# B's weights in fewer, larger loads ahead of GpSimd's compute, and a reordered start, in a four-layer kernel on one core

## The chip, the cores and the metric

One of the eight cores of a Trainium2 chip runs the kernel. The metric is the time of one execution in device microseconds (us), and the number that counts is the median of several runs. Where the text says TensorE, VectorE, ScalarE, GpSimd and SyncE, the profile says PE (and PEld for its weight loads), DVE, ACT, POOL and SP.

## The reference, cut to what matters

Four residual layers run over 2048 rows of 576 numbers: A, B, A, B, with the same weights for both A and for both B. A is attention over a sliding window (8 positions at a distance of 2, 32 heads of 18). B is a recurrence over 64 segments of 32 rows: each segment attends to itself and to 8 memory rows, and the first 8 output rows become the memory of the next segment.

```python
def _B_ref(x, mem0, Wq, Wk, Wv, Wo, seg_len):        # H = 32 heads, Dh = 128
    mem = mem0
    for s in range(n_seg):                            # 64 segments, one after the other
        h = concatenate([mem, x[s * 32:(s + 1) * 32]])
        q, k, v = h @ Wq, h @ Wk, h @ Wv              # 40 rows, 32 heads
        p = softmax(mask(q @ k.T * scale))
        o = einsum("bhte,hed->btd", p @ v, Wo)
        mem = o[:M]
        outs.append(o[M:])

x = x + _A_ref(_layernorm(x), A_wqkv, A_wo)
x = x + _B_ref(_layernorm(x), B_mem0, B_Wq, B_Wk, B_Wv, B_Wo, B_seg_len)
x = x + _A_ref(_layernorm(x), A_wqkv, A_wo)
x = x + _B_ref(_layernorm(x), B_mem0, B_Wq, B_Wk, B_Wv, B_Wo, B_seg_len)
```

All inputs are bf16.

## The kernel before, in words

**Tiling.** A works on tiles of 64 rows (`a_tile`, 32 tiles in each of two layers). B works in 69 steps (`b_step`): step t computes segment t of the first B layer (lane 0) and segment t - 5 of the second (lane 1) in the same matmuls. Each tile of the first A layer feeds two segments of lane 0, and so on, so that all four layers run interleaved.

**Weights.** B's weights stay in SBUF: `wq`, `wk`, `wv` hold rows 0 to 511 of 576, `wqk_r` holds the last 64 rows of both wq and wk, `wv_r` those of wv, and `wo` the output weights; together they are 18.9 MB. A's weights do not fit beside them. They are cut into 12 strips (9 of `A_wqkv`, three each for q, k and v, and 3 of `A_wo`). For the first tile, the strips are loaded into the memory that later holds B's `wo` (L498); so `wo` can only be loaded when tile 0's output projection (L680) has read them. The next two times a strip is needed, it is gathered again from the input, into one of three `ring` buffers; the second of these is also copied to DRAM, and later tiles fetch that copy (L508). A strip is gathered by two DMAs (L504: rows 0 to 511, 512 pieces; L505: the remainder, 64 rows for `A_wqkv`, 128 for `A_wo`).

**What sets the order.** Every operation is given to a planner (`_Plan`) with an engine, a duration, a priority, what it depends on and which buffers it takes. `_Plan.run` walks through a modelled time: on each engine it picks the ready operation with the lowest priority number, and so writes each engine's order of instructions. The engines then run their own lists strictly in order, and wait on semaphores. A planned time has no other effect on the chip. `LAT` and `START` are the planner's assumed latencies and starting times, `PR` its priorities. In the kernel before, B's weight loads are operations of an own queue of the planner, "SWQ": their instructions are issued by GpSimd, but the planner lets a weight load start only when the one before it has moved, and puts it into GpSimd's list at that place, among GpSimd's compute.

**The start.** `setup` first fills constants: GpSimd makes masks and patterns (L298 to L341), VectorE clears tiles (L301 to L401). Then, in the planner's order: SP issues the first x tile (L528), four strips, `B_mem0` (L443) into the same buffer x0, the other eight strips, and the second x tile (L528), again into x0, which must first have been read by the transposes of mem0 (L447). TensorE transposes x (L533), computes LayerNorm's sums (L471), tile 0's q, k and v (L570, 75 matmuls), the logits (L619), then transposes the second x, spreads tile 0's weights (L644), projects tile 0 (L680), and starts step 0 of B with queries and keys (L830 and L833, 27 matmuls for three heads), values (L877), scores (L909 to L919), the product with v (L960) and the projection with `wo` (L984). Tile 1's q, k and v (L570, from the ring) stand in TensorE's list between groups of step 0.

Of the kernel before, what the change touches and what calls it, by code (L numbers as in the profile page):

```python
# [10 lines left out]
ACT = mybir.ActivationFunctionType  # L11
# [5 lines left out]
P = 128  # L17
# [7 lines left out]
NH = 32  # L25
D = 576
T = 64
NS = T // SEG
AH = 32
# [5 lines left out]
EPS = 1e-5  # L35
# [16 lines left out]
class _Plan:  # L52
# [7 lines left out]
    LAT = {"PE": 0.22, "ACT": 0.08, "DVE": 0.08, "POOL": 0.08, "SP": 2.8, "SWQ": 2.2, "NONE": 0.0}  # L60
    SWITCH = 0.1
    PAGE, AHEAD, FETCH, POS = 256, 64, 4.1, 63
    START = {"POOL": 6.0, "SWQ": 6.0, "DVE": 2.5, "ACT": 2.2, "SP": 0.8}
# [183 lines left out]
class _K:  # L247
# [37 lines left out]
    def setup(self):  # L285
        nc, tc = self.nc, self.tc
# [14 lines left out]
        nc.vector.tensor_copy(out=ident4[:].rearrange("p (a b) -> p a b", a=4), in_=ident[:, 0:32].unsqueeze(1).to_broadcast([P, 4, 32]))  # L301
        self.ones = ones = cp.tile([P, P], BF16, name="ones")
        nc.vector.memset(ones[:], 1.0)
        self.ones_h = ones_h = cp.tile([P, P], BF16, name="ones_h")
        nc.vector.memset(ones_h[0:64, :], 1.0)
        nc.vector.memset(ones_h[64:128, :], 0.0)
        self.epsb = epsb = cp.tile([P, 1], F32, name="epsb")
        nc.vector.memset(epsb[:], EPS)
# [9 lines left out]
        et = epadT[0:AH]  # L318
# [6 lines left out]
        for q4 in range(1, 4):  # L325
            nc.vector.tensor_copy(out=epadT[q4 * AH:(q4 + 1) * AH], in_=et)
# [22 lines left out]
        nc.vector.memset(wo[:, NH * D:NH * D + 64], 0.0)  # L349

        st = wo[64:128, 0:9 * 1280].rearrange("p (a b) -> p a b", b=1280).rearrange("p (a c) b -> p a c b", c=3)
        nc.vector.memset(st[:, :, 0:2, 1024:1280], 0.0)
        nc.vector.memset(st[:, :, 2, 512:640], 0.0)
        nc.vector.memset(wo[:, 11 * 1280:12 * 1280], 0.0)
        self.mem0T = mem0T = cp.tile([P, 6, NM], BF16, name="mem0T")
        nc.vector.memset(mem0T[:], 0.0)
# [3 lines left out]
        def tiles(name, n, shape, dt=BF16):  # L360
            ts = [wp.tile(shape, dt, name=f"{name}{i}") for i in range(n)]
            self.pl.pool(name, ts)
            return ts
# [16 lines left out]
        for t_ in tiles("x0", 1, [P, 640]):  # L380
            nc.vector.memset(t_[0:T, D:640], 0.0)
            nc.vector.memset(t_[T:P, :], 0.0)
        tiles("xs", 1, [P, 5, 2, T])
        tiles("st", 1, [P, 2, T], F32)
        for t_ in tiles("xn", 1, [P, 5, T]):
            nc.vector.memset(t_[64:128, 4, :], 0.0)
# [13 lines left out]
        for t_ in tiles("ring", 3, [P, 5 * 256]):  # L400
            nc.vector.memset(t_[64:128, :], 0.0)  # L401
        pp = self.pool("psum", 1, space=PSUM)
        self.pl.pool("r", [pp.tile([P, 512], F32, name=f"r{i}") for i in range(8)])

    def pre(self):
        self.strip_in, self.strip_n = {}, {}

    def prologue(self):

        nc, pl = self.nc, self.pl  # L410
        for name, us in (("xnb1", 0.3), ("hT", 0.4), ("qk", 0.35), ("em", 0.35), ("ex", 0.45), ("fin", 0.3), ("xnb3", 0.3)):
            bufs = [pl.buf(name) for _ in pl.pools[name]]
            o = pl.op("NONE", 0.0, None, -30.0, acq=bufs)
            for b in bufs:
                pl.op("DVE", us, lambda e, b=b: nc.vector.memset(b.t[:], 0.0), -2.5, [o], uses=[b])

        def load(out, in_, mb):
            return pl.op("SWQ", mb / 0.36, lambda e: nc.gpsimd.dma_start(out=out, in_=in_), -20.0)
        o = None
        self.w_in = [[None] * 4 for _ in range(3)]  # L420
        src = (self.B_Wq, self.B_Wk, self.B_Wv)
        for ws in ((0, 1), (2,)):
            for i in ws:
                wr = self.Wb[i][1]
                for hf in range(2):
                    if i < 2:
                        out, in_ = wr[i * 64:(i + 1) * 64, hf * 16 * P:(hf + 1) * 16 * P], src[i][512:576, hf * 16:(hf + 1) * 16]
                    else:
                        out, in_ = wr[hf * 64:(hf + 1) * 64, :], src[i][512:576, hf * 16:(hf + 1) * 16]
                    o = load(out, in_.rearrange("p h e -> p (h e)"), 0.26)  # L430
            for n in range(4):
                for i in ws:
                    w4 = self.Wb[i][0]
                    o = self.w_in[i][n] = load(w4[:, :, n * 1024:(n + 1) * 1024], src[i][0:512, n * 8:(n + 1) * 8].rearrange(
                        "(k p) h e -> p k (h e)", k=4), 1.05)
        self.wo_in = []
        for n in range(4):
            o = load(self.wo[:, n * 8 * D:(n + 1) * 8 * D].rearrange("p (h d) -> p h d", h=8),
                     self.B_Wo[n * 8:(n + 1) * 8].rearrange("h e d -> e h d"), 1.18)
            self.wo_in.append(o)  # L440

        x0, ps = pl.buf("x0"), pl.buf("r")
        a = pl.op("SP", 0.5, lambda e: nc.sync.dma_start(out=x0.t[0:NM, 0:D], in_=self.B_mem0[0]), -2.0, acq=[x0])  # L443

        def tr(e):
            for c in range(5):
                nc.tensor.matmul(ps.t[:, c * NM:(c + 1) * NM], lhsT=x0.t[0:NM, c * P:(c + 1) * P], rhs=self.ident[0:NM, 0:NM],  # L447
                                 start=True, stop=True)
        b = pl.op("PE", 0.3, tr, -2.0, [a], acq=[ps], uses=[x0], mode="R", mm=5)

        def cp(e):
            nc.vector.tensor_copy(out=self.mem0T[:, 0:4, :], in_=ps.t[:, 0:4 * NM].rearrange("p (c n) -> p c n", c=4))
            nc.vector.tensor_copy(out=self.mem0T[0:64, 4, :], in_=ps.t[0:64, 4 * NM:5 * NM])
            nc.vector.tensor_copy(out=self.mem0T[64:128, 5, :], in_=ps.t[0:64, 4 * NM:5 * NM])
        self.mem0_in = pl.op("DVE", 0.6, cp, -2.0, [b], uses=[ps])
# [34 lines left out]
    def wload(self, i, src, rows, col0, n, prio, dep):  # L490
# [3 lines left out]
        pl, dma = self.pl, self.nc.sync.dma_start  # L494
        step, last = rows
# [6 lines left out]
        def gather(e):  # L502
            f, v, r, m = src[0:1, col0:col0 + 1], view(), min(P, src.shape[0] - last), min(n, src.shape[1] - col0)
            dma(out=v[:, 0:4, 0:m], in_=bass.AP(f.tensor, f.offset, [[src.shape[1], P], [step * src.shape[1], 4], [1, m]]))  # L504
            dma(out=v[0:r, 4, 0:m], in_=src[last:last + r, col0:col0 + m])  # L505
# [3 lines left out]
        if k == 0:  # L509
            return view, (), pl.op("SP", 0.9, gather, -2.0 + 0.01 * i, lat=4.0)  # L510
# [5 lines left out]
    def a_tile(self, layer, j, dep, due, span):  # L516

        nc, pl = self.nc, self.pl
# [3 lines left out]
        def pr(f):  # L522
            return due - span * (1.0 - f)
        Q = PR["A"]
        if layer == 1:
# [3 lines left out]
                      pr(0), [dep], acq=[x0])  # L529
# [286 lines left out]
    def qk(self, t, g, prio):  # L816
# [8 lines left out]
        def mm(e):  # L825
            pv = ps.t[:, 0:480].rearrange("p (h w k) -> p h w k", h=3, w=2)
            for hh, h in enumerate(heads):
                for wi in range(2):
# [7 lines left out]
                  {h // 8 for h in heads}] if t == 0 else []), acq=[ps, sb], uses=[hT], mm=9 * n)  # L836
# [17 lines left out]
    def vpass(self, t, k, prio):  # L854
# [12 lines left out]
        for r in range(2):  # L867
            ps = pl.buf("r")

            def mm(e, r=r, ps=ps):  # L870
                for kc in range(5):
                    for c in range(4):
# [6 lines left out]
                      (self.w_in[2][2 * r:2 * r + 2] if t == 0 else []), acq=[ps], uses=[hT, V], mode="C", mm=20)  # L879
# [171 lines left out]
    def trace(self):  # L1051
# [28 lines left out]
        if VERBOSE:  # L1080
# [4 lines left out]
PR = dict(qk=0.388, qkd=0.053, v1=1.358, v0=0.674, w=-0.059, s0=0.051, s1=-1.024, p0=0.894, p1=-0.981, o=0.434,  # L1085
          od=0.001, mo=0.097, xo=1.092, v2=2.128, a1=2.228, a1s=1.274, a2=0.453, a2s=7.821, fin=6.362, res=-5.467,
          ring=-6.659, A=(-0.104, 0.482, 0.742, 0.737, 0.843, -0.012, 0.929, 0.994))
# [61 lines left out]
```

## Time and profile before

| What | us |
|---|---|
| median of 5 runs (2167.55 to 2178.92) | 2172.69 |
| the profiled execution | 2172.35 |
| its span, first to last instruction | 2170.6 |
| TensorE matmuls, busy | 2066.0 |
| VectorE, busy | 1397.2 |
| ScalarE, busy | 1158.1 |
| GpSimd, busy | 940.4 |

The page gives, for the span: the busy time of each engine; the busy share in 40 equal slices; DMA queues; the chain of work that ended last; and the costliest groups. Answers of the trace give the same for any window. An engine name with q (SPq, POOLq) is its sequencer, which issues DMAs. In the DMA queues, q1 is what SP issues (hardware_dynamic) and q0 what GpSimd issues (software_dynamic). Packets also count a few that only signal completion.

### The profile page before, as it was taken

To read this page: it belongs to the slowest core of one execution; us is meant where nothing else is said; L and a number is where in the kernel's file an instruction comes from. 1 tells how busy PE (TensorE), PEld (TensorE's weight loads), DVE (VectorE), ACT (ScalarE), POOL (GpSimd) and SP (SyncE) were. 2 spreads that over 40 slices of the span, in tenths; PEclk is the share of its full clock that TensorE was granted. 3 is DMA by queue.
4 is the path that set the end of the run, shared out by engine and by line. 5 is a ranking of instruction groups with operands and counts; after the bars stand their busy time and mean duration, and the time that the engine had idled before them with its cause. 6 is when DMAs were issued, how large, how long until landed. Compare 5 with 4: busy or idle time off the path is not lost.

```text
span 2170.6 us, 132202 instructions
## 1 busy us (share of the span) xinstructions
PE 2066.0 (95%) x60441; PEld 1727.0 (80%) x60441; DVE 1397.2 (64%) x3541; ACT 1158.1 (53%) x2838; POOL 940.4 (43%) x1338
## 2 busy tenths in 40 slices
PE   1699999999999999999999999999999999999997
PEld 1477888888888888888888888888888888888876
DVE  3467766666666666666766666666666666765675
ACT  1345555555555555555655555555555555655543
POOL 3244444454444445445454454444445445442220
PEclk9899999999999999999999999999999999999999
DMA  7754444443444343333443343443344434332110
GB/s 238 233 174 138 121 121 121 120 129 118 122 125 124 109 134 120 121 113 122 124 122 121 121 136 109 124 122 117 113 133 126 122 111 129 119 119 92 58 57 10
DMA packets 158560, 265.10 MB, mean 122 GB/s; under 512 B 23592, under 2 KB 90032, under 8 KB 158000
## 3 DMA queue, kind: packets, MB, share of 16 engines
q1 hardware_dynamic: 153168, 237.77, 36.1%
q0 software_dynamic: 4832, 18.88, 2.6%
q8 instruction: 472, 7.73, 1.5%
q14 instruction: 88, 0.72, 0.1%
HBM read 240.46 MB, written 16.12 MB: 118 GB/s over the span
## 4 chain that ended last, share of the span: by engine, by line
PE 90%; DMA 4%; DVE 2%; issue 1%; ACT 1%; POOL 1%; SPq 0%; POOLq 0%; ACTq 0%; DVEq 0%
PE r L830 27%; PE r L984 18%; PE r L877 17%; PE r L570 7%; PE r L833 6%; PE r L960 3%; PE r L680 2%; PE r L909 2%; PE r L471 2%; PE r L913 2%; DMA ring<-in_A_wqkv_dram 2%; PE r L644 1%; PE r L919 1%; DMA ring<-strip 1%; PE r L619 1%
## 5 line engine op out<-in xcount | busy, mean ns | idle before, releaser
L830 PE MATMUL r<-hT,wq 128*128 128x80 bf16 (+1 forms) x8832 | 659.5, 198 | 4.9 <-ACT hT L275 2.8
L830 PE MATMUL r<-hT,wk 128*128 128x80 bf16 (+1 forms) x8832 | 661.7, 199 | 0.0
L830 PEld LDWEIGHTS <-wq 128*128 128x128 bf16 x8832 | 500.5, 98 | 32.2 <-issue 22.0
L833 PE MATMUL r<-hT,wqk_r 128*128 128x160 bf16 (+1 forms) x2208 | 507.1, 230 | 0.1
L275 ACT ACTIVATE qk<-r 128x480 bf16<-128x480 f32 (+3 forms) x635 | 333.8, 526 | 237.5 <-PE r L833 225.6
L830 PEld LDWEIGHTS <-wk 128*128 128x128 bf16 x8832 | 446.9, 99 | 0.0
L984 PE MATMUL r<-OT,wo 128*128 128x80 bf16 (+1 forms) x11040 | 417.6, 199 | 17.1 <-issue 10.7
L984 PEld LDWEIGHTS <-wo 128*128 128x128 bf16 x11040 | 394.3, 99 | 34.8 <-issue 24.4
L877 PE MATMUL r<-wv,hT 128*32 128x512 bf16 x5376 | 355.6, 382 | 0.2 <-issue 0.2
L282 POOL TENSOR_TENSOR ex<-ex,sum 128x384 bf16<-128x384 bf16 x138 | 117.4, 850 | 484.4 <-DVE sum L779 336.1
L282 POOL TENSOR_TENSOR big<-qT,kT 128x1024 bf16<-128x1024 bf16 x186 | 310.5, 1689 | 33.0 <-ACT kT L275 22.4
L282 POOL TENSOR_TENSOR big<-big 128x640 bf16<-128x640 bf16 (+1 forms) x59 | 117.7, 1996 | 414.8 <-ACT xs L465 245.4
L275 ACT ACTIVATE V<-r 128x512 bf16<-128x512 f32 x303 | 180.8, 597 | 163.0 <-PE r L877 160.1
L877 PEld LDWEIGHTS <-hT 128*32 128x32 bf16 x6720 | 166.0, 96 | 126.5 <-issue 2.5
L768 DVE TENSOR_REDUCE nmx<-r 128x4 f32<-128x320 f32 (+1 forms) x276 | 143.0, 518 | 148.0 <-PE r L913 145.3
L833 PEld LDWEIGHTS <-wqk_r 128*128 128x128 bf16 x2208 | 219.6, 99 | 0.2 <-issue 0.2
L570 PE MATMUL r<-xn,ring 128*128 128x64 bf16 x4725 | 186.9, 194 | 15.9 <-DMA ring<-in_A_wqkv_dram 12.1
L275 ACT ACTIVATE OT<-r 128x320 bf16<-128x320 f32 (+1 forms) x377 | 138.2, 424 | 103.4 <-PE r L960 103.1
L570 PEld LDWEIGHTS <-ring 128*128 128x128 bf16 x4725 | 161.6, 98 | 39.5 <-issue 17.6
L275 ACT ACTIVATE big<-r 128x384 bf16<-128x384 f32 (+1 forms) x290 | 110.2, 442 | 92.6 <-issue 67.7
L769 DVE TENSOR_TENSOR r<-r,nmx 128x320 f32<-128x320 f32 (+1 forms) x276 | 147.0, 533 | 9.4
L877 PE MATMUL r<-wv_r,hT 128*32 128x512 bf16 x1344 | 133.9, 381 | 0.0
(147 smaller groups left out, 2919.2 us busy)
## 6 DMA issues: line engine op xcount, KB each, us to landing
ring<-strip SPq DMA_DIRECT2D x488, 320.0 KB, 3.4
ring<-strip SPq DMA_DIRECT2D x244, 160.0 KB, 4.0
x1T<-x SPq DMA_DIRECT2D x32, 160.0 KB, 4.2
x<-x1T SPq DMA_DIRECT2D x32, 160.0 KB, 3.9
x3T<-x SPq DMA_DIRECT2D x32, 160.0 KB, 4.5
x<-x3T SPq DMA_DIRECT2D x32, 160.0 KB, 4.2
wo<-in_B_Wo_dram POOLq DMA_DIRECT2D x4, 1152.0 KB, 10.4
wq<-in_B_Wq_dram POOLq DMA_DIRECT2D x4, 1024.0 KB, 15.2
```

Of the source, the lines that this page charges most:

```text
L275: nc.scalar.activation(out=out, in_=in_, func=ACT.Copy, scale=1.0 if scale is None else scale)
L282: (self.nc.vector if e == "DVE" else self.nc.gpsimd).tensor_tensor(out=out, in0=in0, in1=in1, op=op)
L471: nc.tensor.matmul(psf, lhsT=(self.ones if c < 4 else self.ones_h)[:, :], rhs=xs.t[:, c].rearrange("p a t -> p (a t)"), start=(c == 0), st ...
L570: nc.tensor.matmul(ps.t[:, c * T:(c + 1) * T], lhsT=view()[:, kc, w0:w0 + P], rhs=xn.t[:, kc, :], start=(kc == 0), stop=(kc == 4))
L680: nc.tensor.matmul(ps.t[:, mb * T:(mb + 1) * T], lhsT=view()[:, c, w0:w0 + P], rhs=oT.t[:, c, :], start=(c == 0), stop=(c == 4))
L768: nc.vector.tensor_reduce(out=m, in_=v, axis=AX.X, op=ALU.max, negate=True)
L769: nc.vector.tensor_tensor(out=v, in0=v, in1=m.unsqueeze(len(shp) - 1).to_broadcast(shp), op=ALU.add)
L830: nc.tensor.matmul(pv[:, hh, wi, a:b], lhsT=self.Wb[wi][0][:, kc, h * P:(h + 1) * P], rhs=hT.t[:, kc, a:b], start=(hh == 0 and wi == 0 and ...
L833: nc.tensor.matmul(pv[:, hh, :, a:b], lhsT=self.Wb[0][1][:, h * P:(h + 1) * P], rhs=hT.t[:, 4:6, a:b], start=False, stop=(hh == n - 1), sk ...
L877: nc.tensor.matmul(ps.t[c * 32:(c + 1) * 32, :], lhsT=l, rhs=w, start=(kc == 0), stop=(kc == 4))
L960: nc.tensor.matmul(ps[c].t[:, i * n + a - c0:i * n + z - c0], lhsT=V[b].t[q4, r, i, :], rhs=pt.t[q4, i, b, a:z], start=(i == 0 and b == bl ...
L984: nc.tensor.matmul(psY.t[:, mb * W80 + c0:mb * W80 + c1], lhsT=self.wo[:, w0:w0 + P], rhs=self.OT[:, h % 16 // 4 * 8 + h // 16 * 4 + h % 4 ...
```

## The change

- Weight loads are now operations of GpSimd itself, each 0.8 us for the planner, with priority -50: they stand directly behind GpSimd's constants and ahead of all its compute. `wq`, `wk` and `wv` come in two loads each instead of four, `wqk_r` in two instead of four; `wv_r` (two) and `wo` (four, which wait for tile 0) keep their sizes.
- SP's list now begins with the first x tile (priority -30) and then the 12 strips (-20), whose remainders ScalarE issues (only for tile 0's strips); mem0 and the second x come after them.
- VectorE's constants: x0, xn, ones and eps first, epadT last. GpSimd's constants are as before.
- The planner's START for GpSimd and a few priorities are changed, and it now takes GpSimd to be free only at 8.4; with that the first tile's normalized x is computed by VectorE, and TensorE's list in step 0 has all 25 matmuls of tile 1's q in one piece behind 135 of queries and keys, and k and v later. The first transposes of mem0 stand behind tile 0's q, k and v.

```diff
-    LAT = {"PE": 0.22, "ACT": 0.08, "DVE": 0.08, "POOL": 0.08, "SP": 2.8, "SWQ": 2.2, "NONE": 0.0}
+    LAT = {"PE": 0.22, "ACT": 0.08, "DVE": 0.08, "POOL": 0.08, "SP": 2.8, "NONE": 0.0}
...
-    START = {"POOL": 6.0, "SWQ": 6.0, "DVE": 2.5, "ACT": 2.2, "SP": 0.8}
+    START = {"POOL": 8.4, "DVE": 2.5, "ACT": 2.2, "SP": 0.8}
...
+        x0 = self.pl.pools["x0"][0]
+        nc.vector.memset(x0[0:T, D:640], 0.0)
+        nc.vector.memset(x0[T:P, :], 0.0)
+        nc.vector.memset(self.pl.pools["xn"][0][64:128, 4, :], 0.0)
+        nc.vector.memset(ones[:], 1.0)
...
+        for q4 in range(1, 4):
+            nc.vector.tensor_copy(out=epadT[q4 * AH:(q4 + 1) * AH], in_=et)
...
-        def load(out, in_, mb):
-            return pl.op("SWQ", mb / 0.36, lambda e: nc.gpsimd.dma_start(out=out, in_=in_), -20.0)
+        mbs = [2.65]
+
+        def load(out, in_, mb, begin, prio=-50.0):
+            mbs[0] += mb
+            return pl.op("POOL", 0.8, lambda e: nc.gpsimd.dma_start(out=out, in_=in_), prio, lat=max(3.0, 6.5 + mbs[0] / 0.36 - begin))
...
+        for i in range(2):
+            load(self.Wb[i][1][i * 64:(i + 1) * 64, :], src[i][512:576].rearrange("p h e -> p (h e)"), 0.52, 9.2 + 0.8 * n)
+            n += 1
         for ws in ((0, 1), (2,)):
...
+            for hf in range(2):
                 for i in ws:
...
+                    self.w_in[i][hf] = load(self.Wb[i][0][:, :, hf * 2048:(hf + 1) * 2048], src[i][0:512, hf * 16:(hf + 1) * 16].rearrange(
+                        "(k p) h e -> p k (h e)", k=4), 2.1, 9.2 + 0.8 * n)
+                    n += 1
...
+        self.wo_in = [load(self.wo[:, n * 8 * D:(n + 1) * 8 * D].rearrange("p (h d) -> p h d", h=8),
+                           self.B_Wo[n * 8:(n + 1) * 8].rearrange("h e d -> e h d"), 1.18, 36.0, -8.0) for n in range(4)]
...
-            dma(out=v[0:r, 4, 0:m], in_=src[last:last + r, col0:col0 + m])
+            (dma if k else self.nc.scalar.dma_start)(out=v[0:r, 4, 0:m], in_=src[last:last + r, col0:col0 + m])
...
-            return view, (), pl.op("SP", 0.9, gather, -2.0 + 0.01 * i, lat=4.0)
+            o = self.first = pl.op("SP", 0.65, gather, -20.0 + 0.01 * i, lat=4.0)
+            return view, (), o
...
-                      pr(0), [dep], acq=[x0])
+                      pr(0) if j else -30.0, [dep, self.first if j else None], acq=[x0])
...
-PR = dict(qk=0.388, qkd=0.053, v1=1.358, v0=0.674, w=-0.059, s0=0.051, s1=-1.024, p0=0.894, p1=-0.981, o=0.434,
-          od=0.001, mo=0.097, xo=1.092, v2=2.128, a1=2.228, a1s=1.274, a2=0.453, a2s=7.821, fin=6.362, res=-5.467,
-          ring=-6.659, A=(-0.104, 0.482, 0.742, 0.737, 0.843, -0.012, 0.929, 0.994))
+PR = dict(qk=0.388, qkd=0.053, v1=1.358, v0=0.674, w=-0.059, s0=0.001, s1=-1.032, p0=1.109, p1=-0.981, o=0.434,
+          od=0.001, mo=0.162, xo=1.055, v2=2.128, a1=2.228, a1s=1.336, a2=0.453, a2s=7.821, fin=5.91, res=-5.123,
+          ring=-6.622, A=(-0.03, 0.482, 0.785, 0.737, 0.843, -0.012, 0.929, 0.994))
```

The waits of TensorE change with the loads: a head's queries and keys wait for the load of its half (`h // 16`) instead of its quarter (`h // 8`).

## The prediction

> **What bounds the kernel now.** I read the page's slices first, then busy time by stage, the waits of TensorE, the chain, and the DMA queues in short windows.
>
> The slices (one digit is 54 us) show TensorE at 9 tenths in all but the first two and the last one:
>
> ```profile
> PE   1699999999999999999999999999999999999997
> ```
>
> By stage (columns: stage, its length, then busy time and instruction count of PE, PEld, DVE, ACT, POOL, then granted clock, DMA share, GB/s):
>
> ```profile
> 0.00:47.00 47.00, 6.47 (x110) 5.62 (x110) 13.43 (x51) 5.01 (x12) 17.59 (x48) 1.00 0.90 273
> 47.00:63.00 16.00, 4.50 (x65) 3.55 (x66) 9.31 (x27) 5.98 (x18) 0.30 (x2) 1.00 0.15 42
> 63.00:108.00 45.00, 33.10 (x820) 22.92 (x819) 17.58 (x45) 14.54 (x39) 12.31 (x21) 0.81 0.87 268
> ...
> 108.00:2160.00 2052.00, 2017.88 (x59329) 1691.16 (x59330) 1354.53 (x3414) 1131.31 (x2766) 909.42 (x1269) 1.00 0.39 117
> ```
>
> From 108 us on, 59,329 matmuls take 2052 us: 28.9 per us. At that rate the 995 before them are 34 us of work, but they take 108, so about 74 us of the span is start-up loss. The change works there. DMA is busy at 0.90 up to 47 us, idle (0.15) to 63, then busy again at 0.87: two bursts of B's weights with a hole between.
>
> The chain says what is late in each burst (start, length, what):
>
> ```profile
> 22.87 5.95 SPq L505
> 28.92 18.69 DMA x<-in_A_x_dram
> 47.65 0.46 PE r L533 x5
> ...
> 70.35 12.88 DMA ring<-in_A_wqkv_dram
> 83.28 0.81 PE r L570 x10
> 84.09 11.59 DMA ring<-in_A_wqkv_dram
> ```
>
> So the second x tile, 72 KB, lands only at 47.65. TensorE runs in order and waits 24.9 us for it. The path from there to step 0's first query product (63.08) is 15.4 us of small dependent work. Then tile 1's q, k and v strips through the ring arrive late.
>
> Why a small load is late is in the queues (q0: weights, issued by POOL; q1: everything from SP; packets, MB, share). First 24 to 42 us, then 15 to 19, where q1 is alone, then 9.5 to 14.5, while the remainder weights wqk_r load:
>
> ```profile
> q0 software_dynamic: 1584, 6.10, 91.1%
> q1 hardware_dynamic: 1585, 0.62, 13.2%
> ```
> ```profile
> q1 hardware_dynamic: 2409, 0.99, 121.5%
> ```
> ```profile
> q0 software_dynamic: 298, 1.02, 91.6%
> q1 hardware_dynamic: 36, 0.02, 2.3%
> ```
>
> Beside weights, q1 sends exactly one packet per weight packet, 88 per us. Alone it sends 602 per us. A strip's main part is 512 packets, of 128 to 512 bytes: 0.85 us alone, 5.8 us beside weights. The x tile stood in q1 behind the A_wo strips.
>
> **A rule weighed.** The Trainium skill, "DMA: Bandwidth & Descriptors", section "Queues, rings and completion order", says that an engine drains a whole packet, typically 9 to 17 descriptors, from one ring before it switches. By an estimate from that page, with strips in groups of 13, the strips would pass the weights almost unhindered and the second x tile would land near 20 us. The row above, 1585 packets beside 1584, speaks against it, and it is what I use.
>
> **The change, part by part.**
>
> 1. *Constants and first tile.* The first transpose waits till 9.57 for the VectorE memset of xn, queued behind epadT (GpSimd ends that at 5.96) and wo. With x's memsets first (0.33 + 0.09 + 0.09 us) and ident ready at 1.38, it can start when x lands, about 3 us: 6.5 us earlier. The remaining memsets keep VectorE till about 10, so the statistics move from 14.66 to about 10.5. I cost this at nothing: what hides it is the wait for mem0 and the second x. Without that cover it would give 4 us.
>
> 2. *Strips.* SP now issues x, then 12 mains back to back (0.59 us each), then mem0, then the second x. Each HWDGE load uses one of eight semaphores in turn and first waits for the load eight before it; with landings of 3 to 4 us this is no slower than the engines. Mains flow from about 2.7 us. Before the first weight packets, about 9.8 (POOL's first weight issue stays at 8.46), 7.1 us at 602 give 4270 packets, less some 450 of ACT's remainders: 3820 of the 12 x 512 = 6144. Left: 2320, all three A_wo strips and part of v's.
>
> 3. *ACT's remainders.* 12 issues at 0.52 us (row L505) are 6.2 us on ACT, between its evacuations. The remainder of the first A_wo strip waits for that strip's main by its semaphore, and stands ahead of the first tile's Ln on ACT; that of the last stands ahead of the qT evacuation and waits for the second A_wo main. So the first tile's normalization slips to about 20 us, and its q evacuation to about 30. Behind those stand kT, vT and the logits. This too ends before mem0 does, since mem0 is in q1 behind the last A_wo main; with the cover gone it costs up to 10 us. No row shows two HWDGE queues at once. The bounds for the some 510 of its 960 packets left when the weights come: a turn of their own, which costs q1 nothing, or one turn shared with SP's, 510 / 88 = 5.8 us later for the second x. I take the first, since q0 and q1 each have their own turn; by the second, step 0 starts at 63 as now.
>
> 4. *Weights.* 22 loads become 14; eight fewer issues at 0.5 to 0.76 us on POOL are off the path. What counts: wq starts behind wqk_r, at about 14.4, not at 19, and wv follows at once instead of at 64. The first xn goes to VectorE (0.54 + 0.55 us as in rows 53.69 and 54.22), so nothing on POOL waits behind the loads except the four wo loads. These wait on POOL for tile 0's output projection, since wo holds the strips, and the hT copies wait behind them.
>
> **The sum.** *Second x.* 2320 packets at 9.8. Until 14.4, beside wqk_r: between 36 packets in 5 us (7 per us) and the weights' own 60 per us; I take 35, giving 160. The other 2160 at 88 are 24.5 us: 39. Then mem0, its transposes (SP holds the second x until they have read the buffer) and the second x's landing at 2 to 3 us: it lands at about 42, not 47.65. Step 0's first product: 42 + 15.4 = 57.5, not 63.1. *Weights' end.* 18.88 MB in all; 1.05 by 14.4, and 17.83 at 6.10 MB per 18 us is 52.6 us: 67. The wo loads must be issued before the queue runs dry at 53; tile 0's projection ends at 42 + 10.3 = 52, in time. Before, the last wo load was issued at 98.98 and took 6.7. *Tile 1's ring strips.* Issued 2.4 us ahead of step 0 (60.69 and 63.08 now), so from 55; three strips are 1728 packets. Beside weights they get 67 per us (601 in 69 to 78): 12 us give 800, and after 67 the other 930 need 1.5 us. With 1 us to land: 69.5. In the new order TensorE has only 135 query and key matmuls (4.6 us) ahead of all of q's 25, so it stands until then. *After.* k's and v's strips meet no weights; I allow 3 us. From there to step 1's first product are 705 matmuls, 24.4 us: 97. That is the 1040th matmul; in the kernel before, the 995th starts at 108.0 and the 1040th is 1.6 later, 109.6. **Gain: 12.6 us.**
>
> After that the built programs agree: the same 60,441 matmuls, and step 10 begins at the 8715th before and the 8710th after. The TensorE waits after 108.5 us add up to 34 us; the changed priorities reorder them, and I allow 7 either way, taking none. The profiled execution took 2172.35 us (span 2170.6), 0.3 below the median of the runs, 2172.69: 2172.35 - 12.6 is 2160.
>
> A late second x hardly changes this: the end of the weights at 67 sets when tile 1's strips are in. Step 0 at 50 or at 59 gives about the same 97.
>
> **The rivals.**
>
> *Strips ahead of the weights.* If mains and remainders clear before the weights are dense (the weights' first packets ramp slowly: 26 in the first us), the second x lands near 21 and step 0 starts at 36 to 40, when half of wq and wk is in. Ring strips then run from 35 at 67 per us: q by 61, k by 69. From there to step 1 are 617 matmuls, 21.3 us, and 2 for v: 92.5, a gain of 17, 2155. Against it: 6144 packets at 602 need 10 us from 2.7.
>
> *Given back at the ring.* Weights that flow without a hole until 67 starve k and v as they did from 70 to 95, and TensorE's clock, 0.81 over 63 to 108, stays low after the stall: 24.4 / 0.81 is 30, and 3 more for k and v: gain 4, 2168. For it: the hole from 47 to 63 was when nothing needed q1. Against it: in the new order q1's large part comes after the weights. If the loads come no earlier than now, the same time results.
>
> *Slower: starving of q1.* If strips beside the larger loads get the rate seen beside wqk_r, 33 packets in the 2.7 us from 11.7 (12 per us), rather than 88, only some 500 of the 2160 have moved when wq, wk and wv end at 53; the rest needs 3 us alone, and the second x lands at 59. Tile 0's projection, and with it the wo issue, comes at 69, step 0 at 74.5, and wo runs to 83 with q's ring strips starved beside it: in by 87. At the clock of 0.81 the 705 matmuls are 30 us, with 3 for k and v: step 1 at 120, 10 later than now: 2183. The point from which it decides: below 72 per us (2160 packets in the 30 us up to 44.6) the second x is later than now, and below about 57 wo comes so late that the kernel is slower. Against it: from 24 to 42 the rate held at 88 for 18 us.
>
> **How the numbers follow.** Chances: forecast 0.52, strips ahead 0.15, given back 0.23, starving 0.10. A measurement tells 0.3%, 6.5 us, from no change: faster means under 2166.2. Nearly all of the first two and a fifth of the third: 0.70; the rest of the third and a little of the first: 0.20; slower 0.10. Range: from 2150, the strips-ahead case with 5 us of reordering in its favour, to 2172, the given-back case with 4 against it; the starving case is left out.
>
> **What would show it.** The second x lands at 42 (36 to 45), the weights flow without a hole from about 10 to 67, step 0 starts at 57, the first ring strips are consumed by 70, step 1 starts at 97. ACT's Ln of tile 0 is late, at about 20. Wrong if a gap is left in the weights, if q1 runs at another rate than 88 beside them, or if the stage from 108 us on changes by more than 7 us.

## The result, and the profile after

The median fell from 2173.3 us (68 runs) to 2168.79 (39 runs). The ratio is 0.9977, 95% interval 0.9970 to 0.9984: a gain of 5.0 us, between 3.5 and 6.5. The forecast was 12.6. The profiled execution took 2163.85 us (span 2162.2) and gains 8.5 on that of before; single executions of one kernel differ by this much, so below I go by positions inside the traces, and by ratios to the kernel before on the same chip.

The slices of the changed kernel:

```profile
PE   2698999999999999999999999999999999999997
```

The second digit is 6 again: the loss is still in the first 108 us. By stage, in the columns shown for the kernel before:

```profile
0.00:47.00 47.00, 8.58 (x140) 6.94 (x141) 19.66 (x69) 8.86 (x24) 15.62 (x43) 0.83 0.98 320
47.00:63.00 16.00, 7.61 (x170) 7.23 (x169) 4.72 (x14) 3.90 (x11) 2.32 (x4) 0.50 1.03 333
63.00:108.00 45.00, 30.65 (x857) 23.18 (x858) 21.52 (x55) 13.70 (x38) 9.67 (x11) 0.79 0.56 152
108.00:2160.00 2052.00, 2017.20 (x59280) 1692.73 (x59277) 1346.12 (x3389) 1143.10 (x2786) 909.59 (x1267) 1.00 0.38 116
```

The hole in the DMA (0.15 from 47 to 63) is filled (1.03), as the change wants it. Yet by 108 us TensorE has done only 172 matmuls more than before (1167 against 995). The chain says what is late now:

```profile
10.69 22.75 DMA x<-in_B_mem_dram
...
33.80 6.46 DMA x<-in_A_x_dram
...
51.13 8.67 DMA x1T<-x
59.82 0.33 SPq L718
...
62.12 11.87 DMA ring<-in_A_wqkv_dram
...
74.83 4.84 DMA ring<-in_A_wqkv_dram
```

The second x lands at 40.3 and step 0 starts at 55.7, both a little ahead of the forecast. Then tile 1's first strips, issued at 60.2 behind a store and its reload, land at 73 to 74: TensorE stands 12.2 us after the 135 queries and keys. The 1040th matmul comes at 104.4, not at 97 (before: 109.2).

The queues, 24 to 42 us and then 54 to 66, where wo flows:

```profile
q0 software_dynamic: 1713, 6.78, 96.0%
q1 hardware_dynamic: 608, 0.16, 4.0%
q10 hardware_dynamic: 432, 0.15, 3.1%
```
```profile
q0 software_dynamic: 864, 3.71, 93.6%
q1 hardware_dynamic: 297, 0.33, 8.5%
```

From 24 to 42 us the weights run faster than I assumed (6.78 MB, not 6.10); wo runs slower (3.71 MB in 12 us is 0.31 MB per us). ScalarE's remainders have a queue of their own (q10). From 26 to 28 us all three queues have work, and each sends one packet for one of the others:

```profile
q0 software_dynamic: 163, 0.67, 85.2%
q10 hardware_dynamic: 164, 0.08, 13.0%
q1 hardware_dynamic: 164, 0.02, 6.9%
```

### The profile page after: what moved, and what is told of

Its sections match the earlier page's. It is cut to its first block, busy times and chain, and to the rows that moved or that the text cites. A ratio compares the mean times of both kernels' runs of the same rounds, so it can differ in the third digit from the quotient of the medians.

```text
span 2162.2 us, 132233 instructions
## 1 busy us (share of the span) xinstructions
PE 2064.0 (95%) x60441; PEld 1730.1 (80%) x60441; DVE 1392.0 (64%) x3525; ACT 1169.6 (54%) x2859; POOL 937.2 (43%) x1325
## 4 chain that ended last, share of the span: by engine, by line
PE 92%; DMA 4%; DVE 2%; issue 1%; ACT 1%; POOL 0%; SPq 0%; POOLq 0%; ACTq 0%; DVEq 0%
PE r L833 28%; PE r L987 18%; PE r L880 17%; PE r L573 7%; PE r L836 6%; PE r L963 3%; PE r L683 2%; PE r L912 2%; PE r L473 2%; PE r L916 2%; PE r L647 1%; PE r L922 1%; DMA ring<-strip 1%; DMA x<-in_B_mem_dram 1%; PE r L622 1%
## 5 line engine op out<-in xcount | busy, mean ns | idle before, releaser
L275 ACT ACTIVATE qk<-r 128x480 bf16<-128x480 f32 (+3 forms) x659 | 345.7, 529 | 243.5 <-PE r L836 229.0
L880 PE MATMUL r<-wv,hT 128*32 128x512 bf16 x5376 | 354.6, 382 | 0.0
L282 POOL TENSOR_TENSOR big<-big 128x1280 bf16<-128x1280 bf16 (+1 forms) x61 | 122.9, 2015 | 420.4 <-DVE big L282 402.6
L880 PEld LDWEIGHTS <-hT 128*32 128x32 bf16 x6720 | 166.5, 96 | 126.9 <-issue 2.6
L880 PE MATMUL r<-wv_r,hT 128*32 128x512 bf16 x1344 | 133.6, 381 | 0.0
```

The costliest lines, as they stand in the source:

```text
L275: nc.scalar.activation(out=out, in_=in_, func=ACT.Copy, scale=1.0 if scale is None else scale)
L282: (self.nc.vector if e == "DVE" else self.nc.gpsimd).tensor_tensor(out=out, in0=in0, in1=in1, op=op)
L880: nc.tensor.matmul(ps.t[c * 32:(c + 1) * 32, :], lhsT=l, rhs=w, start=(kc == 0), stop=(kc == 4))
```

## The experiments

**Theories.** 1: the missing 7.6 us were lost before step 1. 1a: because SP stands 8.7 us for the store ahead of the ring strips. 1b: because strips beside weights crawl, so that q's strips are in only when the weights end, at 72 instead of 67. 2: the changed priorities give the gain back later. In the table, q is the end of tile 1's q product and 1040 the start of the 1040th matmul, in the profiled execution; the ratio is to the kernel before on the same chip.

| Kernel | median, us | ratio (95%) | step 0 | q | 1040 | weights end |
|---|---|---|---|---|---|---|
| before | 2172.69 | 1 | 63.1 | 72.0 | 109.2 | 105.3 |
| changed | 2168.79 | 0.9977 (0.9970-0.9984) | 55.7 | 75.0 | 104.4 | 72.3 |
| e0_changed_again | 2163.27 | 0.9958 (0.9942-0.9975) | 48.8 | 74.3 | 103.1 | 72.3 |
| e1_old_prio | 2163.08 | 0.9974 (0.9958-0.9990) | 50.4 | 73.8 | 102.4 | 71.4 |
| e2_new_prio | 2166.14 | 0.9998 (0.9982-1.0014) | 63.5 | 71.5 | 112.3 | 108.6 |
| e3_reload_later | 2158.73 | 0.9959 (0.9943-0.9975) | 52.8 | 72.8 | 102.7 | 70.4 |
| e4_less_wo | 2158.97 | 0.9951 (0.9932-0.9970) | 51.2 | 67.9 | 95.9 | 65.1 |
| e5_sp_rem | 2178.04 | 1.0029 (1.0017-1.0041) | 77.6 | 87.3 | 115.7 | 82.0 |
| e6_early_x | 2166.89 | 0.9972 (0.9960-0.9983) | 48.3 | 74.8 | 106.5 | 73.1 |
| e8_wo_behind_ring | 2161.93 | 0.9967 (0.9950-0.9984) | 51.2 | 60.4 | 101.8 | 84.8 |
| e9_wo_behind_v | 2157.40 | 0.9947 (0.9931-0.9962) | 51.1 | 61.0 | 99.7 | 93.1 |
| e12_wo_v_reload | 2155.92 | 0.9940 (0.9925-0.9955) | 54.0 | 60.6 | 99.9 | 93.8 |
| e10_loads_only | 2183.37 | 1.0064 (1.0050-1.0077) | 84.3 | 95.3 | 124.6 | 88.6 |
| e11_start_only | 2152.99 | 0.9920 (0.9903-0.9936) | 42.9 | 65.0 | 93.7 | 89.0 |
| e13_wo_ahead | 2155.35 | 0.9950 (0.9934-0.9965) | 42.4 | 75.4 | 99.5 | 74.0 |
| e14_large_late | 2367.85 | 1.0925 (1.0906-1.0944) | 47.4 | 69.0 | 100.4 | 95.6 |
| e16_old_const | 2164.22 | 0.9985 (0.9974-0.9995) | 57.0 | 75.5 | 103.9 | 72.5 |
| e17_start_old_const | 2153.60 | 0.9933 (0.9916-0.9950) | 43.0 | 65.7 | 94.2 | 89.7 |
| e18_merged | 2152.15 | 0.9931 (0.9911-0.9952) | 42.5 | 64.4 | 92.6 | 88.2 |
| e20_ahead_not_wo | 2148.80 | 0.9914 (0.9894-0.9933) | 48.9 | 63.7 | 92.0 | 87.6 |

**The priorities.** One kernel is the changed one with the old `PR`, the other the kernel before with the new.

> The changed kernel with the old planner priorities (PR) only. Theory 1, the forecast gain was lost in the start (up to step 1): within 2 us of the changed kernel's median of 2168.8, and step 1 still begins at 103 to 106 us. Theory 2, the changed priorities give back in the steady part what the start won: 4 us or more faster than the changed kernel, with the stage from 108 us on shorter by that much.

> The kernel before with the new priorities (PR) only; loads, constants and strips as before. Theory 1: within 2 us of the kernel before. Theory 2: slower than the kernel before by 4 us or more.

The first stands where the changed kernel stands, the second where the one before stands. Theory 2 falls: nothing is given back by the priorities.

**When the ring strips are issued.**

```diff
-                  [dep, (self.x1_stored, self.x3_stored)[lane][j]], acq=[b] if xb is None else [b, xb])
+                  [dep, st], acq=[b] if xb is None else [b, xb])     # lane 0, j 0: st is three empty operations behind the store
...
-                    self.residual(lane, s // NS, self.qk_op.get(t - 1), t + PR["res"])
+                    self.residual(lane, s // NS, self.qk_op.get(t - 1), t + PR["res"] if t else 6.5)
```

> The changed kernel, but on SP's queue the reload of tile 0's residual, which waits 8.7 us for the store ahead of it, stands behind tile 1's first three ring strips. These are then issued at about 52 instead of 60. Theory 1a, SP standing behind the store made the strips late: q's strips are in 7 us earlier (66 instead of 73), step 1 begins at 97 to 99, 5 to 7 us faster. Theory 1b, the end of the weights at 70.5 sets it: strips at one packet per weight packet are in at 70 to 72, step 1 begins 1 to 3 us earlier, 1 to 3 us faster. Theory 2: no difference beyond 1 us.

The chain of this kernel, at the place of the store (SPq L692):

```profile
48.25 0.38 SPq L692
48.68 0.42 SPq L506
...
49.72 22.01 DMA ring<-in_A_wqkv_dram
```

Issued 11 us earlier than in the changed kernel, the last strip still lands at 71.7; it now takes 22 us. That is 1b, and 1a falls. The 1040th matmul is at 102.7 and the ratio 0.9959, as in the repeat of the unaltered kernel, which issues its strips at 50.8 and consumes q at 74.3:

> The changed kernel once more, unaltered, beside the other three on one chip. If its start repeats, step 0 begins at 50 to 56, the weights end at 70 to 72, tile 1's q strips are consumed by 73 to 75 and the 1040th matmul is at 102 to 105. Ratio to the kernel before 0.9970 to 0.9985 as on the record.

Here the second x is in at 33.3 and step 0 starts 7 us earlier than in the first profile, and the 1040th matmul moves by 1.3. Between 48.8 and 55.7, how early step 0 starts hardly counts. (The ratio, 0.9958, is below the 0.9970 that was expected.) The next kernel makes the same point: mem0 goes into `OT`, and both x tiles stand among the strips.

> The changed kernel, but mem0 goes into another buffer and is loaded second on SP, and the second x tile is loaded sixth, among the strips: step 0 begins at 44 to 48, 5 to 8 us earlier than in the changed kernel. Theory 1b: tile 1's q strips are still consumed only at 71 to 74, the 1040th matmul comes 0 to 3 us earlier, the time is 0 to 3 us shorter. Rival, the second x tile sets it: 5 to 8 us shorter.

Its q is in at 74.8 and nothing is won; 1040 is 2 to 3 us later, which neither theory expected and no run explains; the planner also wrote another order of TensorE for it.

**Fewer weights.**

```diff
-        self.wo_in = [load(... h=8), self.B_Wo[n * 8:(n + 1) * 8] ...) for n in range(4)]
+        self.wo_in = [load(... h=hs), self.B_Wo[n * 8:n * 8 + hs] ...) for n, hs in enumerate((4, 4, 4, 8))]
```

> The changed kernel, but the first three of the four loads of B's output weights wo bring 4 heads instead of 8 (heads 4-7, 12-15 and 20-23 are left out and their columns are cleared by VectorE): 1.77 MB less, 5.3 us of weight traffic at the 0.34 MB per us of the middle stage. Theory 1b, the end of the weights sets when tile 1's strips are in: weights end at 65, step 1 begins about 5 us earlier, 4 to 5 us faster. Theory 1a, SP standing behind the store: the store also lands earlier if fewer weights flow beside it, but at most 1 to 2 us; step 1 1 to 2 us earlier. Theory 2: no difference beyond 1 us.

The weights end 7.2 us earlier, q is 6.4 earlier and the 1040th matmul 7.2, against the repeat. In time it is 1.5 us (against the repeat's ratio) to 5.6 us (against the first) ahead, with overlapping intervals, so the time alone decides nothing; the trace shows 1b at the place it speaks of. From the end of tile 1's q to the 1040th matmul are 705 matmuls in both kernels (first the changed one, then this one; columns as above; matmuls still running at the start are counted too):

```profile
74.85:104.44 29.59, 25.56 (x709) 18.24 (x707) 19.62 (x48) 12.14 (x34) 9.67 (x11) 0.88 0.47 120
67.72:95.93 28.21, 25.33 (x708) 18.03 (x706) 19.62 (x48) 12.15 (x34) 9.67 (x11) 0.89 0.48 126
```

They take 28.2 us instead of 29.6, and most of the difference is in waits (2.9 us not busy instead of 4.0). The granted clock is nearly the same, 0.88 and 0.89, so this pair does not tell what the clock is worth. Over 47 to 63 us the changed kernel's clock was 0.50 (the stage's row above). The Trainium skill, "TensorE: Matmul & The Clock Gate", section "HAM oscillation — how this bites in real kernels", counts half of the throttled matmul time as lost. By an estimate from it the 7.61 us busy at a clock of 0.50 in 47 to 63 lost 3.8 us; in this trace they cost nothing, since the 12.2 us wait for strips followed.

**wo behind the strips.** GpSimd first copies eight columns of a ring buffer, so that wo waits for a strip: tile 1's last k strip, then its last v strip, then the latter with the reload moved as above.

```diff
+                    if layer == 1 and j == 1 and part == 1 and c == 4:
+                        seen = pl.op("POOL", 0.1, lambda e, w=w: nc.gpsimd.tensor_copy(out=self.mark[:, 0:8], in_=w[0].t[:, 0:8]), -8.0, [ow], uses=list(w))
+                        for d in self.wo_in:
+                            pl.after(d, seen)
```

> The changed kernel, but the four loads of wo (4.72 MB, 14 us of weight traffic) wait on GpSimd, by a small copy out of the ring, for tile 1's last k strip. wq, wk and wv then end at about 55, and the ring strips of q and k meet no weights. Theory 1b, strips beside weights wait for the weights' end: q consumed by 60 to 62 instead of 73 to 75, k by 66, wo in by 80; the 1040th matmul at 92 to 96 instead of 102 to 105, the time 7 to 10 us shorter than the changed kernel's, if wo is not late for step 0's projection. Rival, the strips are late by SP's wait for the store and by small dependent work: 0 to 3 us shorter. If wo comes late (behind 88), part of it is given back there.

q comes at 60.4, as 1b has it, and k at 66. But the last v strip then stands 13.3 us beside wo, and most of the gain is gone by the 1040th matmul (101.8, and 103.1 in the repeat).

> As the kernel with wo behind the ring, but wo's four loads wait for tile 1's last v strip instead of its last k strip (there the last v strip stood 13.3 us beside wo, and TensorE stood 10.5). Theory 1b: q consumed at 60 to 61, k by 70, v by 73, first values at 76; wo in by 88, so that the projection waits a few us; the 1040th matmul at 92 to 96, 7 to 11 us ahead of the changed kernel, the time 5 to 10 us shorter than the changed kernel's. Rival, what is won at step 1 is given back later (waits behind step 1): 1040th matmul as above, time within 3 us of the changed kernel.

> As the kernel with wo behind the v strips, and on SP the reload of tile 0's residual behind tile 1's q strips: they are issued at 47 to 50, while wv still flows, instead of 53. At 72 packets per us beside weights some 400 of their 1728 packets are then through when wv ends: q consumed 2 to 3 us earlier, the 1040th matmul 0 to 2 us earlier (wo then sets it), the time 0 to 2 us shorter than with wo behind the v strips alone.

TensorE's waits up to 110 us in the kernel with wo behind v (total, times, longest):

```profile
PE r L689 <- DMA ring<-in_A_wo_dram: 5.4, 1, 5.4
...
PE r L579 <- DMA ring<-in_A_wqkv_dram: 4.6, 5, 2.2
```

The 12 to 14 us that TensorE stood for q's strips are gone; what crawls beside wo now is tile 1's A_wo strip (5.4 us), and 1040 is at 99.7, not 92 to 96. In time this is 2.4 us (against the repeat's ratio) to 6.5 us (against the first) ahead of the changed kernel; 5 to 10 were expected. The reload adds nothing that can be told apart. In these three kernels, whatever strip meets wo pays.

**The parts of the change.** ScalarE's remainders are given back to SP; then the weight loads alone are put into the kernel before; then everything but the weight loads.

```diff
-            (dma if k else self.nc.scalar.dma_start)(out=v[0:r, 4, 0:m], in_=src[last:last + r, col0:col0 + m])
+            dma(out=v[0:r, 4, 0:m], in_=src[last:last + r, col0:col0 + m])
```

> The changed kernel, but SP issues the remainders of tile 0's strips itself, as before the change. 24 loads from one queue, 7100 packets: some 2500 of them are left when the weights come, mem0 lands at about 40 and step 0 begins at 58 to 62, 5 or more us later than in the changed kernel. Theory 1b (the end of the weights sets the end of the start): weights end at 70 to 72 all the same, the 1040th matmul within 2 us, the time within 2 us of the changed kernel. Rival, the second x tile sets it: the time 5 us or more longer.

This missed by far: 2178, 14.8 us behind the repeat. The queues from 24 to 42, and the chain:

```profile
q0 software_dynamic: 1601, 6.36, 90.7%
q1 hardware_dynamic: 1601, 0.67, 13.9%
```
```profile
31.02 23.57 DMA x<-in_B_mem_dram
54.95 7.18 DMA x<-in_A_x_dram
```

One packet per weight packet, exactly. The remainders join the queue that must drain at this rate. SP also has two issues per strip, 1.1 us instead of 0.6, so that before the first weights, by 11.3 us, its queue has sent 4026 packets, not 4798. The second x lands at 62.1, step 0 starts at 77.6, and wo, waiting for tile 0, comes so late that the weights end at 82.0.

> The kernel before with the weight loads of the change alone (fewer, larger, ahead of GpSimd's compute; old constants, old order on SP, all remainders by SP, old priorities). SP's queue then meets the weights from 11 us with some 3000 packets left, at 88 to 90 per us: the second x tile lands at 55 to 62, step 0 at 70 to 78 (63 before), wo is issued at 70, the weights end at 80 to 83, the 1040th matmul at 112 to 117 (109 before). 4 to 10 us slower than the kernel before. Rival, weights without GpSimd's compute between them are a gain by themselves: 3 us or more faster than before.

13 us slower than before, more than was expected. SP's queue is still at work on tile 0's strips until 60; step 0 is at 84.3. For these loads the planner also writes another order of TensorE in step 0, with all values behind tile 1's q, k and v, as in the changed kernel; the 13 us are the loads together with that order.

> The changed kernel with the old weight loads (22, issued among GpSimd's compute): constants, strips by SP and ScalarE, and priorities as changed. Strips meet few weights before 20 us; the second x lands before 30, step 0 begins by 45. The weights wait for GpSimd's compute, but that comes earlier too. If the change's gain is the weights' early flow, their end is at 80 to 95 here, the 1040th matmul at 105 to 109, 0 to 4 us faster than before. If it is the reordered start, the 1040th matmul is at 98 to 104 and the time as short as the changed kernel's or shorter.

This overturns what I believed of the change: without its weight loads it gains 17 us, where the whole change gains 5.0 and its repeat 9.1. Here wv is in at 59 and the first load of wo at 63. The other three loads of wo stand on GpSimd behind tile 1's first product, which waits for q and k until 71.96, and are issued at 73.9. So the weights have a hole of some 12 us, and the ring strips pass in it. From 63 to 75 us q0 sends nothing:

```profile
q1 hardware_dynamic: 3545, 1.41, 51.6%
```

The order of TensorE in step 0 is another than in the changed kernel: it depends on the loads' planned times, and here values stand between tile 1's strips.

**Which part of the loads costs.** In the next kernel one thing is changed against the start alone: all of wo is issued directly behind wv.

```diff
+                        "(k p) h e -> p k (h e)", k=4), 1.05, all_wo if i == 2 and n == 3 else None)
...
-            o = load(self.wo[:, n * 8 * D:(n + 1) * 8 * D].rearrange("p (h d) -> p h d", h=8), ..., 1.18)
+            o = load(None, None, 1.18)
```

> The kernel of the start alone (old weight loads), with one thing moved: the last three loads of wo are issued directly behind wv's, ahead of GpSimd's first compute for tile 1, at 47 to 50 instead of 74; TensorE's order is the same. If wo ahead of the ring strips is what the change's loads cost: weights flow without a hole until 72 to 76, k and v strips stand beside them, k is consumed at 75 to 78 instead of 71, v at 80 instead of 77, the 1040th matmul at 97 to 101 instead of 93.7, the time 4 to 7 us longer than the start alone. Rival, the place of wo does not matter (less hole, earlier wo): within 2 us of it.

The wait for tile 1's q, k and v strips up to 110 us, first with wo ahead, then in the start alone:

```profile
PE r L582 <- DMA ring<-in_A_wqkv_dram: 26.2, 6, 11.6
```
```profile
PE r L573 <- DMA ring<-in_A_wqkv_dram: 16.0, 4, 11.2
```

From 63 to 75 us the hole is gone, and SP's queue sends little more than half:

```profile
q0 software_dynamic: 674, 2.88, 71.2%
q1 hardware_dynamic: 1999, 0.85, 33.7%
```

10.2 us more of waiting; q comes at 75.4 and the 1040th matmul at 99.5 instead of 93.7. In time it is 12.5 us ahead of before instead of 17.3; the two intervals just touch. The weights end 15 us earlier than in the start alone, and the kernel is slower.

> The changed kernel's load sizes and their order (14 loads, wqk_r first), but issued among GpSimd's compute as before the change, wo behind tile 1's first compute. If the place of wo is what costs: step 0 at 43 to 47, wo mostly behind 72, the 1040th matmul at 93 to 97, within 3 us of the start alone. If the sizes cost: as the full change, 8 to 10 us longer than the start alone.

This kernel took 2367.85 us, its 1040th matmul is at 100.4 and not at 93 to 97, and it answers nothing about loads: its order of TensorE is another in step 0 too. The planner's modelled times shifted, and it wrote a bad order for the whole run. TensorE's waits behind 110 us:

```profile
PE r L570 <- DMA ring<-strip: 74.2, 63, 2.5
PE r L470 <- ACT xs L464: 22.3, 24, 1.7
```

So the sizes and the place were tried with all other orders kept: the planner still plans 22 small loads, and larger ones are issued in the first one's place, or all ten of wq, wk and wv in front.

```diff
+        front = [remq(0), remq(1)] + [half(i, hf) for hf in range(2) for i in range(2)] + [half(2, 0), half(2, 1), remv(0), remv(1)]
...
+                    o = load(0.26, *front)
+                    front = []
```

> The kernel of the start alone, with the larger loads of the change put into the places of the first of each pair of small ones (wqk_r whole, wq, wk and wv in halves); all other orders stay. Theory, sizes cost nothing: step 0 at 42 to 44, the 1040th matmul within 2 us of 93.7, the time within 2 us of the start alone. Rival, larger loads hold up the strips or step 0: 4 us or more longer.

> The kernel of the start alone, with the change's loads of wq, wk and wv (larger, all issued ahead of GpSimd's compute), but wo in its old place behind tile 1's first compute on GpSimd. The strips meet weights from 11 us, so the second x tile lands at 33 and step 0 begins at 47 to 51 instead of 43, but wv ends at 55 instead of 61 and tile 1's q strips are in by 60 instead of 64. Theory, the place of wo is what costs: the 1040th matmul at 91 to 96, the time within 3 us of the start alone, on either side. Rival, weights ahead of the strips cost the other 4 to 5 us: the 1040th matmul at 97 to 100, 4 us or more longer.

Neither size nor early place costs anything: 15.2 and 18.5 us ahead of before, against 17.3 for the start alone, with overlapping intervals. The second is the fastest kernel of the study: the whole change, but with three of wo's four loads behind GpSimd's first compute for tile 1, and with the order that the planner writes for the old loads' times. Its wait for q, k and v strips, and its stage from 63 us on:

```profile
PE r L578 <- DMA ring<-in_A_wqkv_dram: 8.8, 2, 7.6
```
```profile
63.00:108.00 45.00, 40.58 (x1175) 30.77 (x1173) 28.51 (x71) 22.38 (x64) 12.28 (x15) 0.86 0.61 179
```

40.58 us busy instead of 30.65.

**The constants.**

> The changed kernel with the old order of VectorE's constants (x0, xn, ones and eps behind epadT and wo). The first transpose again waits until 9 to 10 us, tile 0's q until 20. As the forecast has it, the wait for mem0 and the second x hides it: 0 to 1.5 us slower than the changed kernel. Rival, tile 0's chain sets step 0: 4 us slower.

> The start alone (old weight loads) with the old order of VectorE's constants. Here the second x is in before 28 us, so less stands in front of tile 0's chain: by the forecast's price without the cover step 0 begins 3 to 5 us later than 42.9. Since tile 1's q strips stand beside wv's end anyway, I expect 0 to 3 us of it in the time; by the rival, that the second x still hides it, 0 to 1.

The first transpose waits until 9.6 in both, and step 0 moves by 0.1 us in the start alone, not by 3 to 5 (tile 0's q product starts at 16.9 instead of 16.4: it waits for ScalarE and the strips). In time, 0.9 us less is gained than by the changed kernel in the first result (4.3 less than by the repeat), and 3.0 us less than by the start alone; the intervals overlap in each case.

## Why the prediction was wrong in size

- **Second x and step 0** (42, 57.5): 40.3 and 55.7, and 33.3 and 48.8 in the repeat. The first pair is close in part by luck: two errors cancel. The first weights come at 11.3, not at 9.8. In that time SP's queue sends 889 packets more, and then 457 by 14.4, not 160. So from 14.4 on it sends only 1177, not 2160, until mem0 is in at 33.4. Then the second x took 6.5 us beside weights, not 2 to 3. The rate of one packet per weight packet was right (480 beside 482 from 18 to 24 us). That ScalarE's queue takes a turn of its own, so that its remainders cost SP's queue nothing, was right too (163, 164 and 164 packets above); by the other bound the forecast would have had step 0 at 63. Giving them back to SP, with their issues, shows the price of having them in that queue: 77.6. ScalarE's first Ln came at 21.5 (forecast about 20).
- **The weights' end** (67): 72.3. This is the term that failed, and here is where. Besides the later first weights, 0.53 MB, not 1.05, are in by 14.4, with 457 strip packets beside them from 11.3 on. The size of the loads is not the reason: in the kernel with the loads alone the same wqk_r loads, with no strip beside them from 9.5 to 14.5, bring 1.02 MB in these 5 us, as much as the small ones before. From 24 to 42 the rate is 6.78 MB, better than the 6.10 assumed, so that by 48 us 12.2 MB are in, close to the 12.4 of the forecast. From there the last 6.7 MB take 24 us, 0.27 per us, where I had carried 0.339 on. wo's packets (4608 bytes, 221 ns each, 20.8 bytes per ns, against 24.6 for those of 4096 bytes from 24 to 42 us) flow at 0.31 per us, and the last 1.0 MB takes 6.3 us, since 1747 strip packets share the engines with it. I had the row for wo (6.7 us for one load of 1.18 MB, 0.18 per us) and did not use it.
- **Tile 1's ring strips** (issued at 55, 67 per us beside weights, consumed at 69.5): issued at 60.2, consumed at 75.0. I had overlooked that SP stands for the store of x1T, 1.8 us before, 8.7 now, beside weights. But the strips' issue does not matter; 72 packets per us and the weights' end do. That is 5.5 us of the 7.4 missing at step 1.
- **From q to step 1** (24.4 and 3): 29.6. TensorE is busy for 25.6 of it, and 4.0 are waits, of which only 0.9 are for strips. That is 2.2 us more. The 705 matmuls are not a heavier mix than the mean: an estimate from this trace, with the mean interval of each shape from 108 us on, gives 23.3 us. They are slower here, at a granted clock of 0.88 against 1.00 from 108 us on: the 120 of L880 take 73 ns each, there 62. How much of it the clock costs no run shows by itself.
- **The sum**: 97 + 5.5 + 2.2 is 104.7; measured 104.4. Nothing is given back after that: 4.8 us are won at step 1 (109.2 to 104.4; the forecast took 109.6 for the kernel before), 5.0 at the end.
- **"A late second x hardly changes this"**: right between 48 and 57, wrong at 77.6, where it makes wo late.
- **The rivals.** "Given back at the ring" named 2168, and this came, in part by luck: q's strips starved, not k's and v's (0.9 us after q, not 3). Its 30 us for the 705 matmuls at the clock of 0.81 is near the 29.6 measured, but 4.0 of these are waits and the clock there was 0.88. I had given it the lower chance because "q1's large part comes after the weights": it does, and that is the cost, since TensorE waits for it. "Slower" is what the weight loads do without the new order of strips: alone they gave 2183, its number, though not by a lower rate of q1 (1595 packets from 24 to 42 us are 89 per us), but by the 24 loads that stood ahead of the second x.
- **What I had wrong in principle.** I took the hole in the weights for the loss and its filling for the gain. Between q1 and q0 the hole is the time in which the ring passes. The start alone, with a hole, gains 17; wo moved into its hole costs 4.8 us there (5.8 at the 1040th matmul; the intervals of the times just touch).
- **Open.** The changed kernel and the start with wo ahead consume q at the same time (75.0, 75.4), yet the 1040th matmul is at 104.4 (repeat 103.1) and at 99.5. In time that is 5.9 us by the first result's ratio, but 1.7 by the repeat's, within its interval. In the changed order all values stand behind tile 1's q, k and v; in the other they stand between the strips and fill TensorE's waits. That this order is the other part of the cost of the change's loads is argued, not shown: no kernel changed it alone.

## What to carry to other kernels

A queue that is never idle is no gain in itself: list what each transfer holds up, and put the bytes that nobody needs soon (here wo, 14 us of traffic) behind the small strips that an engine waits for. Where two queues alternate by packets, a small-packet load with as many packets as the bulk load beside it takes as long as the bulk, so its time is the bulk's end, not its own issue. And test the parts of a change alone: here one part gained 17 us and the other lost 13 by itself, each with the order that the planner wrote for it.

## What the runs showed that I had not expected

- The wqk_r loads, over 64 partitions, run at 14.6 bytes per ns of an engine's time in packets of 8192 bytes (562 ns each), and at 14.1 in the kernel before in packets of 4096 (290 ns each); packets of 4096 bytes of the other weights run at 24.6 from 24 to 42 us (167 ns each).
- The start of step 0 in one and the same kernel was at 55.7 us in one profiled execution and at 48.8 in another, and the time until the 1040th matmul by 1.3.
- A planner that orders by modelled times can lose 200 us in the steady stage when only its first loads are described otherwise (2153 to 2368 us); larger loads in the places of the small ones, with the order kept, cost nothing (2152).
